# The first nine pairs of an attention-then-mixture kernel: another chunk border, merged mask and add instructions, some row sums on the tensor engine, dummy products, and a new order

## The chip, the cores and the metric

The kernel runs on one core of one Trainium2 chip. The core has five engines with queues of their own: PE (TensorE, matrix products; its weight loads are shown as PEld), DVE (VectorE), ACT (ScalarE), POOL (GpSimd) and SP (SyncE, which here only issues DMAs). The metric is device time in microseconds, from the first to the last instruction of one execution; the median of several executions is compared. All times below are microseconds (us) unless marked ns.

## The reference

Two attention layers follow each other. The first has 8 batches of 8 heads, 576 positions and head width 64, with a bias made of running sums; the second takes its output (576 x 512 per batch) through four experts, each a causal attention of head width 64, and adds the two experts that a gate picks.

```
scores = scale * q @ k.T ; s_pos = max(s, 0) ; cum = cumsum(s_pos)
scores = where(causal, -1e9, scores + min(-(cum_i - cum_j), 0))
attn = exp(scores - rowmax) ; attn /= sum(attn) + 1e-9 ; out = attn @ v
...
logits = x @ w_gate ; two largest per row, softmax of the two -> w
for e in range(4):
    q, k, v = x @ wq[e], x @ wk[e], x @ wv[e]
    a = softmax(causal(scale * q @ k.T)) ; ye = a @ v @ wo[e]
    out += (w of e, where picked) * ye
```

## The kernel before

Work goes by **pairs**: two heads of the first layer, or two experts of the second, are one pair, and there are 50 slots, 48 of which hold a pair (`pairs`). Pairs 0 to 3 are batch 0 of the first layer, 4 to 7 batch 1; pairs 8 and 9 are batch 0 of the second layer; then the pattern (four and two) repeats every six slots.

For one pair the steps are these. `hi` (h0 to h3, hc) makes the rounded copies Q2 and K2 on ACT. `maxima` (m0 to m5, tiles mx, L488) computes bf16 scores on PE, and M0 to M5 (L502) reduces them to row maxima on DVE, ten reductions a pair, each with a read of the accumulator. `minus_max` (mt, mA, mq) turns the maxima on PE (L522), copies them on ACT (L526) and sends them by DMA into a row of Q2. `lo` (lq, lk, l0 to l3) makes the low parts Q1 and K1: copies on POOL (L446, first three pairs) or by DMA, on ACT (L455, first nine pairs), and subtractions on DVE (L463, L468; those of pair 1 on POOL). `scores` (s0 to s6, L549 and L554) computes transposed scores in three chunks of 512 columns and a tail, for two heads each; E0 to E6 (L570, L581) is the exponential on ACT into the tile p (two buffers, pairs take turns). `below` (d0 to d3, all on POOL) masks the diagonal blocks with L591 and adds the key blocks up into r (L602 to L616), so that one product with ones gives row sums later (`sums`, L698, copied by L707). `pv` (v0 to v7, L647) is the product with the values on PE, copied out by V0, V1 (L661). `recip` and `norm` divide, and `projections` (L874) are the second layer's products.

Every engine takes its instructions strictly in the order in which the program issues them, so the order decides what waits for what. That order is written out by hand as a list of `slot:step` words: FILLING (up to slot 9), MIDDLE (six slots, repeated five times) and DRAINING. A step of slot n works for pair n (scores), n-1 (pv, sums), n+1 (maxima 3 to 5, low parts) or n+2 (maxima 0 to 2, hi). PE's results go to eight banks, which `take` and `give` hand round in that order.

Of the kernel before, what the change touches and what calls it, by code (L numbers as in the profile page):

```python
# [177 lines left out]
def order():  # L178

    def listed(text, n0=0):  # L180
        for x in text.split():
            n, step = x.split(":")
            yield n0 + int(n), step
# [997 lines left out]
```

## Time and profile before

| | |
|---|---|
| median of 3 runs | 666.05 us (663.31 to 669.95) |
| profiled execution, first to last instruction | 663.4 us |
| PE / PEld busy | 96% / 80% |
| DVE / ACT / POOL busy | 84% / 68% / 68% |
| granted clock of PE, mean | 0.993 |

The profiled execution is one of its own; its span is its time, there is nothing outside it, and it lies inside the range of the runs, 2.7 us under their median. Busy shares are of the whole span. A busy PE is not PE at its peak, since the ends of products are modelled. Queries of the trace by stretch, line, wait and time follow in the section of rows.

### The profile page before, as it was taken

The numbers are of one execution on the slowest core, as the hardware profiler recorded it, in microseconds if no ns is written. First come the engines' busy times: TensorE is split into PE (matmuls) and PEld (weight loads), VectorE is DVE, ScalarE is ACT, GpSimd is POOL, SyncE is SP. The second block draws the span as 40 slices with busy tenths as digits, with TensorE's granted clock in tenths as the row PEclk, the third lists the DMA queues.
The fourth block names the chain that finished last, engine by engine and source line by source line (L and its number), as shares of the span: only waits on it lengthen the run. The fifth ranks groups of instructions, "written<-read, shape, count | busy, mean of one in ns | idle before, by whom it ended". The sixth has DMA issues, their size and how long they took to land.

```text
span 663.4 us, 16171 instructions
## 1 busy us (share of the span) xinstructions
PE 637.9 (96%) x5792; PEld 528.1 (80%) x5792; DVE 559.4 (84%) x1446; ACT 454.3 (68%) x983; POOL 451.3 (68%) x611
## 2 busy tenths in 40 slices
PE   3889899999999999999999999999999999999997
PEld 1665698797897888788888888878887888779885
DVE  6889897998989898988989899897989976681985
ACT  6578868677667776777668766677767767566464
POOL 9889768678758667766786686686677766837030
PEclk9989999999999999999999999999999999999999
DMA  4435343544544473445643555535634543421323
GB/s 144 129 92 158 112 134 83 140 127 120 156 128 121 128 190 86 125 120 148 174 105 105 156 131 144 135 115 142 184 90 127 144 121 79 122 78 36 92 65 112
DMA packets 52157, 81.21 MB, mean 122 GB/s; under 512 B 18430, under 2 KB 26622, under 8 KB 52078
## 3 DMA queue, kind: packets, MB, share of 16 engines
q1 hardware_dynamic: 52078, 80.18, 44.5%
q8 instruction: 46, 0.75, 0.5%
q14 instruction: 33, 0.27, 0.1%
HBM read 44.55 MB, written 10.09 MB: 82 GB/s over the span
## 4 chain that ended last, share of the span: by engine, by line
PE 78%; DVE 9%; DMA 5%; ACT 4%; SPq 1%; issue 1%; DVEq 0%; ACTq 0%
PE pvp L647 15%; PE pq L874 13%; PE s L549 10%; PE s L554 10%; PE mx L488 8%; PE pw L874 8%; PE po L874 6%; PE sm L698 3%; DVE mx L502 3%; DVE k L468 1%; DMA q<-mr 1%; DVE pv L765 1%; PE po L850 1%; DMA k<-cum 1%; ACT k L431 1%
## 5 line engine op out<-in xcount | busy, mean ns | idle before, releaser
L502 DVE CUSTOM_DVE_ANT_0 mx<-mx,mask 128x64 f32<-128x64 f32 (+7 forms) x432 | 184.8, 445 | 42.5 <-PE mx L488 30.6
L570 ACT ACTIVATE p<-s 128x512 f32<-128x512 f32 x288 | 161.7, 594 | 66.8 <-PE s L554 62.5
L591 POOL TENSOR_SCALAR_AFFINE_SELECT p<-p 128x256 f32<-128x256 f32 (+1 forms) x240 | 124.1, 518 | 105.6 <-ACT p L570 96.9
L549 PE MATMUL s<-q,k 128*128 128x256 f32 (+3 forms) x672 | 175.1, 290 | 3.0 <-DVE mcol L502 2.4
L554 PE MATMUL s<-q,k 97*128 97x256 f32 (+3 forms) x672 | 164.8, 286 | 3.3 <-DMA q<-mr 3.2
L549 PEld LDWEIGHTS s<-q,k 128*128 128x128 f32 (+1 forms) x672 | 125.5, 187 | 13.3 <-issue 2.6
L613 POOL TENSOR_TENSOR r<-r,p 128x640 f32<-128x640 f32 x92 | 129.0, 1402 | 7.7
L554 PEld LDWEIGHTS s<-q,k 97*128 97x128 f32 (+1 forms) x672 | 124.7, 187 | 5.9 <-DMA q<-mr 4.7
L488 PE MATMUL mx<-k,q 96*64 96x320 bf16 (+7 forms) x960 | 97.5, 307 | 13.5 <-DMA k<-p 11.3
L647 PE MATMUL pvp<-p,v 128*64 128x320 f32 (+4 forms) x1024 | 105.6, 337 | 0.4 <-ACT mr L526 0.4
L463 DVE TENSOR_TENSOR q<-raw,q 64x576 fp32r<-64x576 f32 x94 | 84.2, 903 | 25.8 <-ACT q L428 11.9
L647 PEld LDWEIGHTS pvp<-p,v 128*64 128x64 f32 x1024 | 65.6, 137 | 32.1 <-issue 2.5
L468 DVE TENSOR_TENSOR k<-raw,k 64x576 fp32r<-64x576 f32 x94 | 86.3, 925 | 3.1 <-DMA k<-k 0.6
L488 PEld LDWEIGHTS <-q 96*64 96x64 bf16 x960 | 47.7, 114 | 42.3 <-issue 12.1
L874 PE MATMUL pq<-xh,wqkh 128*128 128x288 f32 x256 | 77.7, 303 | 0.1
L874 PE MATMUL pq<-xl,wqkh 128*128 128x288 f32 x256 | 75.5, 295 | 0.0
L874 PE MATMUL pq<-xh,wqkl 128*128 128x288 f32 x256 | 75.5, 295 | 0.0
L608 POOL TENSOR_TENSOR r<-p 128x256 f32<-128x256 f32 x46 | 36.3, 789 | 54.4 <-ACT p L570 53.8
L428 ACT ACTIVATE q<-raw 64x576 fp32r<-64x576 f32 x96 | 64.6, 679 | 6.7 <-DMA raw<-in_qk_dram 5.6
L502 DVE DVE_READ_ACCUMULATOR2_ANT mcol<- 128x1 f32 x480 | 65.7, 137 | 0.8
L431 ACT ACTIVATE k<-raw 64x576 fp32r<-64x576 f32 x96 | 64.3, 680 | 1.8
L661 ACT ACTIVATE pv<-pvp 128x256 f32<-128x256 f32 (+1 forms) x92 | 36.6, 406 | 28.4 <-PE pvp L647 28.4
(133 smaller groups left out, 1201.5 us busy)
## 6 DMA issues: line engine op xcount, KB each, us to landing
raw<-in_qk_dram SPq DMA_DIRECT2D x30, 576.0 KB
rb<-rr SPq DMA_DIRECT2D x92, 144.0 KB
q<-q SPq DMA_DIRECT2D x45, 288.0 KB
k<-k SPq DMA_DIRECT2D x39, 288.0 KB
v<-in_vm_dram SPq DMA_DIRECT2D x32, 256.0 KB
out_dram<-o SPq DMA_DIRECT2D x32, 256.0 KB
q<-mr SPq DMA_DIRECT2D x96, 2.2 KB
raw<-in_qk_dram SPq DMA_DIRECT2D x4, 288.0 KB
```

The lines of the kernel that those rows point to most:

```text
L431: nc.scalar.activation(k2[0:64, j], get_raw(n, j)[64:128], AF.Copy)
L463: eng.tensor_tensor(a[64:128, j], get_raw(n, j)[0:64], q2[0:64, j].bitcast(F32), op=OP.subtract)
L468: eng.tensor_tensor(c[0:64, j], get_raw(n, j)[64:128], c[64:128, j].bitcast(F32), op=OP.subtract)
L488: nc.tensor.matmul(t[64 * j : 64 * j + 64, c0 : c0 + k1 - k0], q2[0:RC, 64 * qt : 64 * qt + 64], k2[0:RC, k0:k1], start=True, stop=True,)
L502: nc.vector.tensor_tensor_reduce(t[:, c0 : c0 + w], t[:, c0 : c0 + w], mask[:, m0 : m0 + w], scale=1.0, scalar=mcol[n][:, 9:10] if slot == ...
L549: nc.tensor.matmul(t[0:nk, c0 : c0 + q1 - q0], K1[r1(n)][:, j, k0 : k0 + nk], Q1[r1(n)][:, j, q0:q1], start=True, stop=False,)
L554: nc.tensor.matmul(t[0:nk, c0 : c0 + q1 - q0], K2[r2(n)][0 : RM + 1, j, k0 : k0 + nk], Q2[r2(n)][0 : RM + 1, j, q0:q1], start=False, stop= ...
L570: nc.scalar.activation(ptile[n][:, x % 2, 512 * ci : 512 * ci + 512], tl[x], AF.Exp, scale=0.125)
L591: nc.gpsimd.affine_select(out=a, in_=a, pattern=[[0, 2], [1, nk]], compare_op=OP.is_ge, fill=0.0, base=0, channel_multiplier=-1,)
L613: add(r[:, :, q0:S], r[:, :, q0:S], p[:, :, 1024 + c : 1024 + c + S - q0], op=OP.add)
L647: nc.tensor.matmul(cur[h][64 * j : 64 * j + 64, q0 - PVC[h] : q1 - PVC[h]], vsl(j, kt), ptile[n][:, j, c : c + q1 - q0], start=first, stop ...
L874: nc.tensor.matmul(t[0:nk, 0:w], l, r, start=(x == 0), stop=(x == len(terms) - 1))
```

## The change

It touches the first nine pairs (EARLY = 9), and one thing in all pairs.

- Chunks: in pairs 0 to 8 the first two chunks of scores end at query column 320, not 256 and 576/384 (`EARLY_SCHUNKS`), and the value product's halves meet at 320 too. Columns in total stay the same.
- p is laid out anew: the two heads of a chunk lie beside each other, so that both diagonal masks of a chunk, for both heads, are one instruction (four blocks of 128). The third chunk's masks are merged so in every pair; the first chunk's in pairs 0 to 8.
- Adds: in pairs 0 to 8 the first chunk has one add (two heads of 192) and the second one (two of 256). The copy of the first 128 columns into r is a step of its own, e0: on POOL in pairs 0 to 3, on ACT in 4 to 8.
- Row sums: in pairs 0 to 3 (SUMMED = 4) POOL doesn't add the third chunk and the tail; PE sums r, the third chunk and the tail by products with ones (`early_sums`, b0), and ACT copies them out (B0). `sums` of those pairs falls away.
- Low parts: in pairs 0 to 8 both heads are one instruction (l0 and l1; l2 and l3 fall away). The K copy of pairs 3 to 8 moves from ACT to POOL, one instruction of 64 x 1152.
- Two fills of ring 0 move from POOL to DVE; the identity, the ones, gw and tlt move into unused columns of p.
- Dummy products: 12 of 256 columns before everything else and 48 of 64 columns (z0 to z47) spread over slots -2 to 4, all into one bank that is held until `zz`.
- Order: one list, STEPS. From 10:mq on it equals the old order word for word, apart from words that name no step.

```diff
+EARLY_SCHUNKS = [
+    [(0, 0, 320, 0), (1, 128, 320, 320)],
+    [(0, 320, 576, 0), (1, 320, 576, 256)],
+    [(2, 256, 576, 0), (3, 384, 576, 320)],
+]
+EARLY = 9
+SUMMED = 4
+FIRST_IDLE, IDLE = 12, 48
...
         def copy_k():
-            if n < COPY_K:
+            if COPY_Q <= n < COPY_K:
+                nc.gpsimd.tensor_scalar(
+                    c[64:128], get_raw(n, slice(0, 2))[64:128], 1.0, 0.0, op0=OP.mult, op1=OP.add
+                )
+            elif n < COPY_K:
...
-        for j in range(2):
+        parts = (slice(0, 2),) if n < EARLY else (0, 1)
+        for x, j in enumerate(parts):
...
+        def two_diags(ci):
+            base = PCHUNK[ci][0]
+            lower(p[:, base : base + 1280].rearrange("p (b c) -> p b c", c=320)[:, :, 0:128], 128)
...
+            if ci == 0 and n < EARLY:
+                two_diags(0)
+                add(r[:, :, 128:320], chunk_of(0, 128, 320), chunk_of(0, 320, 512), op=OP.add)
...
+            elif ci == 1 and n < EARLY:
+                add(r[:, :, 320:S], chunk_of(1, 0, 256), chunk_of(1, 256, 512), op=OP.add)
...
+                two_diags(2)
+                if n >= SUMMED:
+                    for kt, q0, _, c in chunks(n)[2]:
+                        add(r[:, :, q0:S], r[:, :, q0:S], chunk_of(2, c, c + S - q0), op=OP.add)
...
+        def early_sums():
+            t = tl[7] = take(f"es{n}")
+            r = rtile[n]
+            for h, (a, z) in enumerate(((0, 384), (384, S))):
+                parts = [(r, a, z)] + [
+                    (heads(p, at, c, c + q1 - q0), q0, q1)
+                    for kt in (2, 3, 4)
+                    for q0, q1, at, c in pieces(n, kt, max(KT[kt][0], a), z)
+                    if q0 < q1
+                ]
+                for x, (src, q0, q1) in enumerate(parts):
+                    for j in range(2):
+                        o = 64 * h + 32 * j
+                        rows = src[:, j, q0:q1] if x == 0 else src[:, j]
+                        nc.tensor.matmul(
+                            t[o : o + 32, q0 - a : q1 - a], ones[:, 0:32], rows,
+                            start=x == 0, stop=x == len(parts) - 1, tile_position=(0, o),
+                        )
...
+    def idle(k, cols=64):
+        if not idle_bank:
+            idle_bank.append(take("idle"))
+        w, m = (ident, P) if k % 2 else (ones, D)
+        nc.tensor.matmul(
+            idle_bank[0][0:m, 0:cols], w, ones[:, 0:1].to_broadcast([P, cols]),
+            start=True, stop=True,
+        )
...
+    for k in range(FIRST_IDLE):
+        idle(0, 256)
     running_sums()
```

How instructions stand on two engines, at the places of which the prediction speaks. On POOL, the work of pair 2 on its exponentials (tile p, buffer 0; r2 are its sums; k1 is the low part of K). Before:

```order
L608 TENSOR_TENSOR r2_672<-p0_106 128x2x128
L609 TENSOR_TENSOR r2_672<-p0_106 128x2x192
L591 AFFINE_SELECT p0_106<-p0_106 128x2x128
L613 TENSOR_TENSOR r2_672<-r2_672,p0_106 128x2x320
L591 AFFINE_SELECT p0_106<-p0_106 128x2x128
L613 TENSOR_TENSOR r2_672<-r2_672,p0_106 128x2x192
L591 AFFINE_SELECT p0_106<-p0_106 128x2x128
L602 TENSOR_SCALAR r2_672<-p0_106 128x2x128
L591 AFFINE_SELECT p0_106<-p0_106 128x2x128
L606 TENSOR_TENSOR r2_672<-p0_106 128x2x128
L591 AFFINE_SELECT p0_106<-p0_106 64x2x64
L616 TENSOR_TENSOR r2_672<-r2_672,p0_106 64x2x64
```

And in the changed kernel, from pair 2's first add on, to the start of pair 3 (p1):

```order
L744 TENSOR_TENSOR r2_718<-p0_74 128x2x192
L753 TENSOR_TENSOR r2_718<-p0_74 128x2x256
L715 AFFINE_SELECT p0_74<-p0_74 128x4x128
L735 TENSOR_SCALAR r2_718<-p0_74 128x2x128
L573 TENSOR_SCALAR k1_0_66<-raw4_427 64x1152
L715 AFFINE_SELECT p1_75<-p1_75 128x4x128
```

Six adds are two, four masks are two (the first stands just ahead of these rows), and the K copy of pair 4 now stands between pair 2 and pair 3.

On DVE, the start of the program, from the end of the running sums. Before:

```order
L298 TENSOR_TENSOR p1_107<-s_c_124,p1_107 64x576
L468 TENSOR_TENSOR k1_0_66<-raw0_130,k1_0_66 64x576 x2
L502 ISA mx0_0_145,mcol0_164<-mx0_0_145,mask_86 128x448
L502 ISA mcol0_164 128x1
L502 ISA mx0_0_145,mcol0_164<-mx0_0_145,mask_86 128x64
```

And in the changed kernel:

```order
L417 TENSOR_TENSOR p1_75<-s_c_133,p1_75 64x576
L592 TENSOR_TENSOR k1_0_66<-raw0_139,k1_0_66 64x1152
L587 TENSOR_TENSOR q1_0_64<-raw0_139,q2_0_68 64x1152
L627 ISA mx0_1_168,mcol0_192<-mx0_1_168,mask_86 128x384
L627 ISA mcol0_192 128x1
```

The low part of Q of pair 0 has moved ahead of the first maxima; before, it stood behind all ten of pair 0 and two of pair 1.

## Rows read from the trace of the kernel before

**Rows 1.** Busy time by stretch: us, engines (instructions), granted clock, DMA share, GB/s.
```profile
12.20:32.90 20.70, 18.09 (x98) 12.44 (x95) 17.18 (x62) 12.00 (x22) 17.52 (x34) 1.00 0.49 143
...
43.20:50.00 6.80, 6.80 (x41) 4.36 (x39) 5.50 (x15) 3.62 (x8) 4.93 (x7) 0.50 0.34 105
...
12.20:151.00 138.80, 131.36 (x1137) 102.28 (x1135) 121.62 (x325) 102.34 (x211) 108.87 (x150) 0.98 0.45 124
151.00:280.00 129.00, 128.50 (x1237) 108.46 (x1233) 117.14 (x298) 89.71 (x199) 94.04 (x121) 1.00 0.49 132
```

**Rows 2.** Waits from 12.2 to 151 us: us in total, times, longest.
```profile
DVE mx L502 <- PE mx L488: 8.4, 9, 2.0
```

**Rows 3.** Timeline of PE, parts up to 151 us: start, us, instruction, idle before.
```profile
10.78 3.28 PE L488 MATMUL mx<-k,q 96*64 96x448 bf16 x20 [10.78 <-DMA k<-p]
...
32.16 0.41 PE L549 MATMUL s<-q,k 128*128 128x256 f32 x1
32.37 0.41 PE L554 MATMUL s<-q,k 97*128 97x256 f32 x1
...
33.00 0.28 PE L549 MATMUL s<-q,k 128*128 128x256 f32 x1
33.12 0.28 PE L554 MATMUL s<-q,k 97*128 97x256 f32 x1
...
41.45 0.42 PE L554 MATMUL s<-q,k 97*128 97x320 f32 x1 [0.86 <-DMA q<-mr]
...
151.21 1.08 PE L488 MATMUL mx<-k,q 96*64 96x512 bf16 x12
```

**Rows 4.** Timeline of DVE, 9 to 52 us.
```profile
9.60 0.75 DVE L468 TENSOR_TENSOR k<-raw,k 64x576 fp32r<-64x576 f32 x1
12.24 0.63 DVE L502 CUSTOM_DVE_ANT_0 mx<-mx,mask 128x448 f32<-128x448 f32 x1 [1.89 <-PE mx L488]
...
18.31 2.63 DVE L463 TENSOR_TENSOR q<-raw,q 64x576 fp32r<-64x576 f32 x2
...
26.81 0.50 DVE L502 CUSTOM_DVE_ANT_0 mx<-mx,mask 128x320 f32<-128x320 f32 x1 [1.96 <-PE mx L488]
...
30.39 0.70 DVE L502 CUSTOM_DVE_ANT_0 mx<-mx,mask 128x512 f32<-128x512 f32 x1 [0.79 <-PE mx L488]
...
43.98 0.70 DVE L502 CUSTOM_DVE_ANT_0 mx<-mx,mask 128x512 f32<-128x512 f32 x1 [1.11 <-PE mx L488]
...
50.44 1.59 DVE L468 TENSOR_TENSOR k<-raw,k 64x576 fp32r<-64x576 f32 x1
```

**Rows 5.** Timeline of POOL, 41 to 51 us (pairs 1 and 2).
```profile
41.32 0.73 POOL L608 TENSOR_TENSOR r<-p 128x256 f32<-128x256 f32 x1 [0.66 <-ACT p L570]
42.01 1.01 POOL L609 TENSOR_TENSOR r<-p 128x384 f32<-128x384 f32 x1
42.98 0.41 POOL L591 TENSOR_SCALAR_AFFINE_SELECT p<-p 128x256 f32<-128x256 f32 x1
43.47 1.55 POOL L613 TENSOR_TENSOR r<-r,p 128x640 f32<-128x640 f32 x1
...
50.42 1.00 POOL L609 TENSOR_TENSOR r<-p 128x384 f32<-128x384 f32 x1
```

**Rows 6.** Groups on POOL by shape, whole run: count, busy us, mean ns, idle before.
```profile
L591 POOL TENSOR_SCALAR_AFFINE_SELECT p<-p 128x256 f32<-128x256 f32 x192 | 101.7, 530 | 96.9 <-ACT p L570 96.9
...
L616 POOL TENSOR_TENSOR r<-r,p 64x128 f32<-64x128 f32 x48 | 27.4, 572 | 8.2 <-DVE r L613 4.3
L602 POOL TENSOR_SCALAR r<-p 128x256 f32<-128x256 f32 x48 | 23.9, 498 | 4.2
...
L446 POOL TENSOR_SCALAR q<-raw 64x576 fp32r<-64x576 f32 x6 | 5.0, 842 | 0.2
```

**Rows 7.** Timeline of PE, 51 us: half of a quad's row sums, and what follows.
```profile
51.20 0.69 PE L698 MATMUL sm<-r,ones 128*32 128x288 f32 x8
51.83 0.65 PE L647 MATMUL pvp<-p,v 128*64 128x256 f32 x4
```

More of the change, by code (lines that the diff above doesn't have):

```diff
@@ L33, with chunks, pv_cols, pieces @@
 ]
-PCOLS = 1600
-LASTQ = [(0, 256), (256, 384), (384, 576)]
-PVC = [0, 256, 576]
-PT = 1536
-def pieces(kt, q0, q1):
+EARLY_SCHUNKS = [
[3 rows of a table added]
+]
+EARLY = 9
+SUMMED = 4
+FIRST_IDLE, IDLE = 12, 48
+PCHUNK = [(1152, 640), (2304, 512), (0, 640)]
+PTAIL = (512, 64)
+PSPARE = 1152 + 512
+PCOLS = 3328
+LASTQ = [(0, 256), (256, 384), (384, 576)]
+def chunks(n):
+    return EARLY_SCHUNKS if n < EARLY else SCHUNKS
+def pv_cols(n):
+    return [0, 320, 576] if n < EARLY else [0, 256, 576]
+def pieces(n, kt, q0, q1):
     if kt == 4:
-        return [(q0, q1, PT + q0 - 512)]
+        return [(q0, q1, PTAIL, q0 - 512)]
     out = []
-    for ci, segs in enumerate(SCHUNKS):
+    for ci, segs in enumerate(chunks(n)):
         for k, a, z, c in segs:
@@ L48, in pieces, with heads @@
             if k == kt and lo < hi:
-                out.append((lo, hi, 512 * ci + c + lo - a))
+                out.append((lo, hi, PCHUNK[ci], c + lo - a))
     return out
+def heads(t, at, c0, c1):
+    base, width = at
+    t = t[:, base : base + 2 * width].rearrange("p (j c) -> p j c", c=width)
+    return t[:, :, c0:c1]
 MBANKS = [
@@ L61 @@
 ]
-FILLING = (
[39 rows of a table removed]
-)
-MIDDLE = (
[24 rows of a table removed]
-)
-DRAINING = (
[43 rows of a table removed]
+STEPS = (
[213 rows of a table added]
 )
 def order():
[L180 to L183, printed above, removed]
-    yield from listed(FILLING)
-    for n0 in range(10, 40, 6):
-        yield from listed(MIDDLE, n0)
-    yield from listed(DRAINING)
+    for x in STEPS.split():
+        n, step = x.split(":")
+        yield int(n), step
 COPY_Q, COPY_K = 3, 9
@@ L215, in tile_attention_then_moe, with fill @@
     K2 = [const.tile([P, 2, S], F32R, tag=f"k2_{i}", name=f"k2_{i}") for i in range(NQK2)]
-    def fill(*rings):
-        for i in rings:
-            nc.gpsimd.memset(K2[i][64:96].bitcast(F32), 0.0)
-        for i in rings:
-            nc.gpsimd.memset(Q2[i][64:96].bitcast(F32), 1.0)
-        for i in rings:
-            nc.gpsimd.memset(K2[i][96:128].bitcast(F32), 1.0)
+    def fill(i):
+        eng = nc.gpsimd if i else nc.vector
+        eng.memset(K2[i][64:96].bitcast(F32), 0.0)
+        eng.memset(Q2[i][64:96].bitcast(F32), 1.0)
+        nc.gpsimd.memset(K2[i][96:128].bitcast(F32), 1.0)
+    PB = [const.tile([P, PCOLS], F32, tag=f"p{i}", name=f"p{i}") for i in range(2)]
+    ones = PB[1][:, PSPARE : PSPARE + D]
+    nc.vector.memset(ones, 1.0)
     fill(0)
-    ident = const.tile([P, P], F32, tag="ident", name="ident")
+    ident = PB[0][:, PSPARE : PSPARE + P]
     make_identity(nc, ident)
-    ones = const.tile([P, D], F32, tag="ones", name="ones")
-    nc.vector.memset(ones, 1.0)
+    gw = PB[1][:, PSPARE + D : PSPARE + D + 5 * E].rearrange("p (t e) -> p t e", e=E)
     eps = const.tile([P, 1], F32, tag="eps", name="eps")
@@ L254, in tile_attention_then_moe @@
     zL = const.tile([P, 2, P], F32R, tag="zl", name="zl")
-    PB = [const.tile([P, 2, PCOLS], F32, tag=f"p{i}", name=f"p{i}") for i in range(2)]
     VB = [const.tile([P, 2, 5, D], F32, tag=f"v{i}", name=f"v{i}") for i in range(3)]
     vx = const.tile([P, 5, 260], F32, tag="vx", name="vx")
-    gw = const.tile([P, 5, E], F32, tag="gw", name="gw")
-    tlt = const.tile([P, 5, E, E], BF16, tag="tlt", name="tlt")
+    tlt = PB[1][:, PSPARE + D + 5 * E : PSPARE + P - 4].bitcast(BF16)
+    tlt = tlt.rearrange("p (t a b) -> p t a b", a=E, b=E)
     tgt = const.tile([P, 5, E, E], BF16, tag="tgt", name="tgt")
@@ L266, in late_constants @@
         for i in range(2):
-            nc.gpsimd.memset(PB[i][64:128, :, PT:PCOLS], 0.0)
+            nc.gpsimd.memset(heads(PB[i], PTAIL, 0, 64)[64:128], 0.0)
         for i in range(3):
@@ L564, in chunk @@
             t = tl[x] = bank(x)
-            for kt, q0, q1, c0 in SCHUNKS[x // 2]:
+            for kt, q0, q1, c0 in chunks(n)[x // 2]:
                 seg(t, x % 2, kt, q0, q1, c0)
@@ L570, in exp @@
             nc.scalar.activation(
-                ptile[n][:, x % 2, 512 * ci : 512 * ci + 512], tl[x], AF.Exp, scale=0.125
+                heads(ptile[n], PCHUNK[ci], 0, 512)[:, x % 2], tl[x], AF.Exp, scale=0.125
             )
@@ L581, in exp_tail @@
             nc.scalar.activation(
-                ptile[n][0:64, :, PT:PCOLS],
+                heads(ptile[n], PTAIL, 0, 64)[0:64],
                 tl[6][0:64, 0:128].rearrange("p (j c) -> p j c", c=64), AF.Exp, scale=0.125,
@@ L585, in exp_tail, with lower @@
             give(tl[6])
-        def diag(kt):
-            nk = KT[kt][1]
-            (_, _, c), = pieces(kt, KT[kt][0], KT[kt][0] + nk)
-            a = ptile[n][0:nk, :, c : c + nk]
+        p = ptile[n]
+        def lower(a, w):
             nc.gpsimd.affine_select(
-                out=a, in_=a, pattern=[[0, 2], [1, nk]], compare_op=OP.is_ge,
+                out=a, in_=a, pattern=[[0, a.shape[1]], [1, w]], compare_op=OP.is_ge,
                 fill=0.0, base=0, channel_multiplier=-1,
             )
-        def below(ci):
+        def two_diags(ci):
+            base = PCHUNK[ci][0]
+            lower(p[:, base : base + 1280].rearrange("p (b c) -> p b c", c=320)[:, :, 0:128], 128)
@@ L597, in below, with chunk_of, sums_of, first @@
+        def chunk_of(ci, c0, c1):
+            return heads(p, PCHUNK[ci], c0, c1)
+        def sums_of():
             if n not in rtile:
                 rtile[n] = sb.tile([P, 2, S], F32, tag="r", name=f"r{n}", bufs=3)
-            p, r = ptile[n], rtile[n]
-            if ci == 0:
-                diag(0)
+            return rtile[n]
+        def first():
+            r, a = sums_of()[:, :, 0:128], chunk_of(0, 0, 128)
+            if n < SUMMED:
+                nc.gpsimd.tensor_scalar(r, a, 1.0, 0.0, op0=OP.mult, op1=OP.add)
+            else:
+                nc.scalar.activation(r, a, AF.Copy)
@@ L602, in below @@
+        def below(ci):
+            if ci < 2 or n >= SUMMED:
+                r = sums_of()
+            if ci == 0 and n < EARLY:
+                two_diags(0)
+                add(r[:, :, 128:320], chunk_of(0, 128, 320), chunk_of(0, 320, 512), op=OP.add)
+            elif ci == 0:
+                lower(chunk_of(0, 0, 128), 128)
                 nc.gpsimd.tensor_scalar(
-                    r[:, :, 0:128], p[:, :, 0:128], 1.0, 0.0, op0=OP.mult, op1=OP.add
+                    r[:, :, 0:128], chunk_of(0, 0, 128), 1.0, 0.0, op0=OP.mult, op1=OP.add
@@ L604, in below @@
                 )
-                diag(1)
-                add(r[:, :, 128:256], p[:, :, 128:256], p[:, :, 256:384], op=OP.add)
+                lower(chunk_of(0, 256, 384), 128)
+                add(r[:, :, 128:256], chunk_of(0, 128, 256), chunk_of(0, 256, 384), op=OP.add)
+            elif ci == 1 and n < EARLY:
+                add(r[:, :, 320:S], chunk_of(1, 0, 256), chunk_of(1, 256, 512), op=OP.add)
             elif ci == 1:
-                add(r[:, :, 256:384], p[:, :, 512:640], p[:, :, 384:512], op=OP.add)
@@ L609, in below @@
[L609 removed]
+                add(r[:, :, 256:384], chunk_of(1, 0, 128), chunk_of(0, 384, 512), op=OP.add)
+                add(r[:, :, 384:S], chunk_of(1, 128, 320), chunk_of(1, 320, 512), op=OP.add)
             elif ci == 2:
[L611 to L617 removed]
+                two_diags(2)
@@ new lines, in below @@
+                if n >= SUMMED:
+                    for kt, q0, _, c in chunks(n)[2]:
+                        add(r[:, :, q0:S], r[:, :, q0:S], chunk_of(2, c, c + S - q0), op=OP.add)
+            else:
+                a = heads(p, PTAIL, 0, 64)[0:64]
+                lower(a, 64)
+                if n >= SUMMED:
+                    nc.gpsimd.tensor_tensor(r[0:64, :, 512:S], r[0:64, :, 512:S], a, op=OP.add)
+        def early_sums():
[16 more added lines that the diff above has]
+                        )
@@ L618, in below, with early_copy @@
+        def early_copy():
+            m = n | 1
+            if m not in rs:
+                rs[m] = sb.tile([P, S], F32, tag="rs", name=f"rs{m}", bufs=1)
+            o = 64 * (n % 2)
+            for h, (a, z) in enumerate(((0, 384), (384, S))):
+                nc.scalar.activation(
+                    rs[m][o : o + 64, a:z], tl[7][64 * h : 64 * h + 64, 0 : z - a],
+                    AF.Identity, bias=eps[0:64],
                 )
+            give(tl[7])
         for x in range(6):
@@ L625, in scores @@
             items[f"d{ci}"] = lambda ci=ci: below(ci)
+        if n < EARLY:
+            items["e0"] = first
+        if n < SUMMED:
+            items["b0"] = early_sums
+            items["B0"] = early_copy
         return items
@@ L632, in pv @@
         ph, b, i = pairs[n]
+        PVC = pv_cols(n)
         items = {}
@@ L648, in piece @@
                     cur[h][64 * j : 64 * j + 64, q0 - PVC[h] : q1 - PVC[h]],
-                    vsl(j, kt), ptile[n][:, j, c : c + q1 - q0],
+                    vsl(j, kt), heads(ptile[n], at, c, c + q1 - q0)[:, j],
                     start=first, stop=fin,
@@ L669, in pv @@
                 for kt in kts
-                for q0, q1, _ in pieces(kt, max(KT[kt][0], PVC[h]), PVC[h + 1])
+                for q0, q1, *_ in pieces(n, kt, max(KT[kt][0], PVC[h]), PVC[h + 1])
             ]
@@ L687, in sums @@
     def sums(n):
-        if n not in quads:
+        if n not in quads or n < SUMMED:
             return {}
@@ L1127, in slot @@
                     steps.update(norm(z))
+        if n == -2 and IDLE:
+            for k in range(IDLE):
+                steps[f"z{k}"] = lambda k=k: idle(k)
+            steps["zz"] = lambda: give(idle_bank[0])
         if n == -1:
```

16 lines of the change are left out of this document (5 added, 11 removed), and 319 rows, old and new, of tables (DRAINING, FILLING, MIDDLE, STEPS).

## Prediction

> **What bounds the kernel now.** I read the busy time by stretch first. From 151 to 280 us PE is busy 128.50 of 129.00 us: the repeating middle part is paced by PE, nothing in it hangs on absolute time, and the order there is unchanged. So whatever the first slots win or lose arrives at the end one to one, and only the stretch up to about 151 us, where the new order meets the old one (10:mq; the first products behind it are in a group that starts at 151.21 us [rows 3]), has to be priced. In that stretch, 12.2 to 151 us, no engine is full: PE 131.36 of 138.80, DVE 121.62, POOL 108.87, ACT 102.34 [rows 1]. But PE's busy time is stretched. Products of 256 columns start 0.21 us apart at 32.2 us and 0.12 us apart at 33.0 us [rows 3]: up to about 32.9 us, from the first product at 10.78 us on [rows 3], PE ran at the lower of its two levels, 1.2 GHz, though the column of the granted clock says 1.00 for that stretch (no record of it was kept). From 43.2 to 50 us the granted clock is 0.50, the lower level again, and PE is busy all the 6.80 us [rows 1]; before that fall it had waited 0.86 us for a DMA [rows 3]. DVE is the engine with the least to spare behind it: 88% busy here, against 91% (117.14 of 129.00) in the steady part [rows 1]. Of its 17.2 us of idle time, 8.4 are waits for the maxima's products on PE [rows 2], and the rows of its timeline show where: 1.96 and 0.79 us at 26.8 and 30.4 us, 1.11 at 44.0, all in the two stretches at 1.2 GHz, and 1.89 us at 12.2 us, ahead of the first maxima [rows 4]. POOL is idle for 30 of the 138.8 us [rows 1] and is not last at the meeting point. My reading: DVE paces slots 0 to 5 and PE, by its projections, the rest, with the slow clock as the common cause of DVE's larger gaps.
>
> **The change, part by part.** I price it by DVE's time up to the meeting point, and then ask whether PE and POOL follow.
>
> Start on DVE. The Q low part of pair 0 moves ahead of the first maxima, into the 1.89 us in which DVE waited for PE. Uncontended, a 64x576 subtraction takes 0.75 us [rows 4], so two take 1.5 us, and they fit. Later, where the two stood, 2.63 us come free [rows 4], of which 1.1 us were contention that may come back elsewhere. I take 1.5 us won (0 to 1.9).
>
> Clock. The dummy products are to keep PE at 2.4 GHz from its first real product. If they do, the three DVE waits of 1.96, 0.79 and 1.11 us go: 3.9 us (0 to 3.9, and to 8.4 if all waits on PE went).
>
> Low parts. Eight pairs (0 and 2 to 8; pair 1's run on POOL) have two DVE instructions where four stood: 16 fewer. What one costs beside its elements: the reductions of 320 and 512 columns take 0.50 and 0.70 us [rows 4], which is 1.04 ns a column, so 576 columns are 0.60 us, and 0.15 of the 0.75 us is fixed. 16 x 0.15 = 2.4 us. The slope is that of another operation; ends 0 and 4.8 us (twice the fixed part).
>
> POOL. In pairs 0 to 3 the adds of 0.73 (L608), 0.73 (L606, same size), 1.01, 1.55, 1.01 and 0.57 us, 5.6 us, become one of 1.01 (two of 192) and one of two of 256: from 0.73 at 256 and 1.01 at 384 elements, 1.29 at 512. That is 3.3 us a pair, 13.2 in four. In pairs 4 to 8, 0.73 + 0.73 + 1.01 become 2.3 and a copy of 0.50 us goes to ACT: 0.7 a pair, 3.3. A double mask has no row; between 0.41 (no dearer) and 0.82 I take 0.6, so 0.2 saved twice a pair, 3.6 us in nine. Against it six K copies of 64x1152: two of L446 would be 1.7 us; 1.5 each, 9 us [rows 5, 6]. POOL's 108.87 us fall by about 11. With its 30 us of idle time this is cover and not gain: it lets value products of pairs 0 to 3 start earlier, and I price it at nothing by itself (0 to 3 us). What is queued behind each K copy are the next pair's masks, and behind those PE's value products; 1.5 us six times is less than the 13 us taken off ahead of them.
>
> ACT loses 12 K copies and gets five copies and some more sum copies; with 36 us idle [rows 1] it stays off the path. Nothing.
>
> PE. Half a quad's row sums, 288 columns with four groups side by side, hold PE 0.63 us (51.20 to 51.83) [rows 7]: 2.2 ns a column. A pair's early sums stream 1152 columns a head: 2.5 us if only the two heads run side by side, half if all four groups do. Four pairs: 5 to 10 us, less the two quads' old sums (2 x 2 x 0.63 = 2.5): 2.5 to 7.6 more. The dummies of 64 columns cost 0.14 us each at that price; some 40 stand behind the first real product: 5.6 us. The 12 of 256 columns are 0.56 us each, 6.7 us, twice that at the lower level; they run before 10.78 us, where PE had nothing to do [rows 3], and at worst delay the first maxima by about 2 us. So PE gets at most 13 us more, and the clock gives back half of what was busy at the lower level: 18.09 / 2 + 6.80 / 2 = 12.4 us [rows 1]. The two cancel; I take 0, with ends 0 and 6 us lost. One bank of eight is held by the dummies up to slot 4; no row prices that, and I put it into the same ends.
>
> Everything behind slot 10: the third chunk's masks are merged in all pairs, but POOL waits there anyway (96.9 us idle ahead of L591 in the whole run, for exponentials [rows 6]): nothing.
>
> The port. At 50.44 us a DVE subtraction took 1.59 us instead of 0.75 beside a POOL add that had started at 50.42 and took 1.00 [rows 4, 5]: it waited for about that add's end. Half as many DVE subtractions and less POOL work mean fewer such meetings, six K copies mean new ones; I take 0, from 2 won to 9 lost. The Trainium skill, "SBUF — State Buffer", section "SBUF: two separate sides", calls the pair of ports that VectorE and GpSimd share an exclusive lock, held for the whole instruction, for a VectorE operation with two SBUF inputs against a GpSimd one that reads SBUF; the trace agrees in this row (0.84 us lost of 1.00). By that rule moving copies from ACT to POOL speaks against this change; the second rival below is what it would make.
>
> **Sum.** 1.5 + 3.9 + 2.4 = 7.8 us off the profiled execution's 663.4, so 655.6. That execution is one run, 2.7 us under the median of the three shown, so against the median: 666.05 - 7.8 = 658.
>
> **Rivals.** 1% of 666 is 6.7 us, about what a measurement of this kernel can tell from no change, since its runs spread from 663.3 to 670.
>
> Forecast: DVE closes its gaps, 658 us, own range 653 to 661. For it: the gaps are named and two of the three causes are removed. Against it: the gaps of one order are replaced by those of another, and a kernel whose first slots have four engines at 74 to 95% seldom loses a gap without growing one.
>
> The port takes it back: each of the six K copies on POOL (1.3 to 1.7 us) stands close to the DVE subtraction that reads it, in the neighbouring pair's work. If every one blocks a subtraction of the other stream for its length, 9 us are lost; for half of them 4.5: 666.05 - 7.8 + 4.5 = 663. For it: the 1.59 and 2.63 us rows. Against it: two operations must meet in time, and of the rows of 0.75 us and more [rows 4] one ran at 9.60 us undisturbed.
>
> The change doesn't do what it says: the sparse dummies don't keep the clock up, the waits of 3.9 us stay: 662. For it: PE fell to the lower level at 43.2 us after a stretch with only short waits; between the first maxima and the first scores, 12 to 20 us, the new PE queue is still sparse.
>
> Slower: PE becomes the engine that paces slots 0 to 4. The place is PE's queue, where sums and dummies stand ahead of products that are ready. At the lower level the 13 us added are 26; nothing is given back; what PE had free in the stretch is 7.4 us (138.80 - 131.36), and DVE then waits, so its savings are worth nothing: 26 - 7.4 = 19 us, 685. It decides from the point where the added time less what the clock returns is over 7.4 us. Against it: at 2.4 GHz the difference is under 1 us.
>
> **How the numbers follow.** Forecast 0.50, the port 0.23, the clock 0.20, slower 0.07. The first is faster by over 1%, the next two within 1%, the last slower: 0.50, 0.43, 0.07. The range: at best DVE is 95% busy, (121.6 - 2.4) / 0.95 = 125.5 us instead of 138.8, 13.3 won, and with the runs' spread 651; at the other end both middle rivals together, and half of PE's bound, 668.
>
> **What the profile would show.** If right: products of 256 columns 0.12 us apart from the first scores on and no stretch with a granted clock of 0.50; the group of maxima's products at the meeting point (151.21 us before) near 143.5; DVE's waits for the maxima's products before it under 5 us; POOL's busy time up to there near 98 us; the span behind it unchanged within 2 us. The prediction is wrong if DVE's waits name another cause in the same size, if subtractions on DVE average well over 2 x 0.75 us for both heads, or if the part behind the meeting point gets longer.

## The result and the profile after

| | before | after |
|---|---|---|
| median of 15 runs | 667.96 us (663.31 to 669.95) | 662.12 us (660.07 to 666.38) |
| ratio | | 0.9917, 95% interval 0.9898 to 0.9937 |
| profiled execution | 663.4 us | 662.1 us |

The change wins 5.8 us. That is clear of the noise, and with 0.8% it is below the 1% that I had named as what can be told from no change. A run's time and its profiled span are not the same: the profiled run of after is listed with 663.8 us and spans 662.1, and in all runs with both numbers the time is 1.7 to 2.2 us above the span. So something lies outside the span, and a span of 663.4 us stands for a run of before of about 665.1, 2.9 us under its median and among its fastest; the one of after lies 1.7 us over its median. The two profiles differ by only 1.3 us. A comparison of the two shows what the fill became, and not where the medians part.

The windows of after that answer to [rows 1] (us, engines with instructions, granted clock), and three more, cut where its clock changes:

```profile
12.20:32.90 20.70, 20.70 (x130) 16.41 (x125) 14.21 (x49) 10.56 (x20) 12.29 (x9) 0.59 0.26 68
43.20:50.00 6.80, 6.80 (x67) 5.94 (x63) 6.08 (x10) 5.80 (x13) 2.96 (x4) 1.00 0.64 209
12.20:151.00 138.80, 135.50 (x1261) 114.60 (x1255) 115.66 (x308) 99.01 (x207) 90.40 (x105) 0.93 0.46 123
151.00:280.00 129.00, 128.68 (x1245) 109.02 (x1245) 114.09 (x294) 89.56 (x199) 91.29 (x113) 1.00 0.48 129
...
12.40:29.30 16.90, 16.90 (x91) 13.20 (x87) 10.75 (x44) 7.67 (x15) 8.68 (x6) 0.50 0.22 58
29.40:142.00 112.60, 109.30 (x1107) 92.30 (x1107) 96.09 (x244) 85.58 (x182) 77.30 (x94) 1.00 0.50 134
142.10:145.40 3.30, 3.30 (x18) 3.30 (x17) 3.23 (x11) 1.96 (x4) 3.03 (x4) 0.50 0.79 200
```

The record of the clock begins at 5.5 us, at 2.4 GHz, while the first burst of dummies runs, and falls at 12.3 us, just behind the first maxima (11.10 us). Then PE is busy all of 16.90 us, dummies included, and all of it at 1.2 GHz. Behind that, one fall of 3.3 us is left up to 151 us. POOL is down to 90.40 us from 108.87, DVE to 115.66 from 121.62. PE is up by only 4.1 us. DVE, which was to close its gaps, has more of them: 23.1 us idle of the 138.8 where before had 17.2. PE has 3.3 where it had 7.4.

The timeline of PE in after, parts up to the meeting point, answers to [rows 3]:

```profile
20.54 0.45 PE L1273 MATMUL idle<-p 128*64 128x64 f32 x2
...
22.57 0.48 PE L1273 MATMUL idle<-p 128*64 128x64 f32 x2
22.98 0.64 PE L674 MATMUL s<-q,k 128*128 128x320 f32 x1
...
28.00 0.41 PE L674 MATMUL s<-q,k 128*128 128x256 f32 x1
28.21 0.41 PE L679 MATMUL s<-q,k 97*128 97x256 f32 x1
...
32.54 0.28 PE L679 MATMUL s<-q,k 97*128 97x256 f32 x1
32.66 0.28 PE L674 MATMUL s<-q,k 128*128 128x256 f32 x1
...
152.18 1.34 PE L613 MATMUL mx<-k,q 96*64 96x448 bf16 x16
```

Five dummies hold PE for 2.44 us (20.54 to 22.98) directly ahead of pair 0's first scores, which came at 19.21 us in the trace of before. Products of 256 columns are still 0.21 us apart at 28.0 us, 0.12 at 32.5. The group of pair 12's maxima at the meeting point starts at 152.18 us (151.21 before), but the two groups do not hold the same products. The first scores of pair 12 do, in before and then in after:

```profile
168.03 0.31 PE L549 MATMUL s<-q,k 128*128 128x320 f32 x1
169.77 0.31 PE L674 MATMUL s<-q,k 128*128 128x320 f32 x1
```

They come 1.7 us later in after, and from them to the end it is 495.3 and 492.3 us. So in this pair of profiles the fill has won nothing, and what is won lies behind it.

DVE in after, timeline (answering to [rows 4]) and then its longest waits from 12.2 to 151 us (to [rows 2]; total, times, longest):

```profile
9.34 1.41 DVE L592 TENSOR_TENSOR k<-raw,k 64x1152 fp32r<-64x1152 f32 x1 [0.33 <-ACT k L578]
10.78 1.35 DVE L587 TENSOR_TENSOR q<-raw,q 64x1152 fp32r<-64x1152 f32 x1
12.43 0.57 DVE L627 CUSTOM_DVE_ANT_0 mx<-mx,mask 128x384 f32<-128x384 f32 x1 [0.29 <-PE mx L613]
...
29.41 2.48 DVE L587 TENSOR_TENSOR q<-raw,q 64x1152 fp32r<-64x1152 f32 x1 [5.63 <-ACT p L695]
```
```profile
DVE q L587 <- ACT p L695: 5.6, 1, 5.6
DVE mx L627 <- PE mx L613: 3.5, 4, 1.7
DVE wol L436 <- ACT woh L435: 3.4, 1, 3.4
```

The waits for the maxima's products fell from 8.4 to 3.5 us as hoped. A new one stands in their place: Q's low part of pair 2 needs the ring of two to be read out by pair 0's scores. The last of those starts at 29.12 us, and DVE's queue stands behind it. (The row names an exponential on ACT as what came last; the readers of the ring are the scores.)

### The profile page after: what moved, and what is told of

The parts are those of the page before. It is cut to its first block, busy times and chain, and to the rows that moved or that the text cites. A ratio compares the mean times of both kernels' runs of the same rounds, so it can differ in the third digit from the quotient of the medians.

```text
span 662.1 us, 16453 instructions
## 1 busy us (share of the span) xinstructions
PE 650.7 (98%) x5976; PEld 547.3 (83%) x5976; DVE 558.2 (84%) x1432; ACT 450.3 (68%) x980; POOL 424.4 (64%) x530
## 4 chain that ended last, share of the span: by engine, by line
PE 81%; DVE 7%; DMA 4%; ACT 3%; issue 2%; SPq 1%; DVEq 0%; ACTq 0%
PE pvp L832 16%; PE pq L1058 12%; PE s L674 11%; PE s L679 10%; PE pw L1058 9%; PE mx L613 9%; PE po L1058 7%; PE sm L882 3%; DVE mx L627 3%; PE idle L1273 1%; DMA rb<-rr 1%; ACT p L695 1%; DVE pv L949 1%; DMA raw<-in_qk_dram 1%; PE po L1034 1%
## 5 line engine op out<-in xcount | busy, mean ns | idle before, releaser
L715 POOL TENSOR_SCALAR_AFFINE_SELECT p<-p 64x128 f32<-64x128 f32 (+2 forms) x183 | 111.7, 611 | 117.8 <-ACT p L695 103.2
L674 PE MATMUL s<-q,k 128*128 128x320 f32 (+3 forms) x672 | 173.5, 288 | 2.3 <-DVE mcol L627 2.2
L679 PE MATMUL s<-q,k 97*128 97x320 f32 (+3 forms) x672 | 163.8, 285 | 0.6 <-DMA q<-mr 0.6
L761 POOL TENSOR_TENSOR r<-r,p 128x640 f32<-128x640 f32 x84 | 118.0, 1405 | 6.8
L587 DVE TENSOR_TENSOR q<-raw,q 64x576 fp32r<-64x576 f32 (+1 forms) x86 | 82.8, 971 | 25.7 <-ACT q L547 11.9
L832 PE MATMUL pvp<-p,v 128*64 128x192 f32 (+4 forms) x1024 | 102.2, 334 | 0.8 <-DVE mcol L627 0.8
L613 PE MATMUL mx<-k,q 96*64 96x448 bf16 (+6 forms) x960 | 92.6, 300 | 1.8 <-DMA k<-p 0.9
L592 DVE TENSOR_TENSOR k<-raw,k 64x576 fp32r<-64x576 f32 (+1 forms) x86 | 87.1, 1020 | 2.6 <-ACT k L578 0.3
L755 POOL TENSOR_TENSOR r<-p 128x256 f32<-128x256 f32 x37 | 28.9, 780 | 52.6 <-ACT p L695 52.1
L846 ACT ACTIVATE pv<-pvp 128x320 f32<-128x320 f32 (+1 forms) x92 | 36.4, 405 | 27.5 <-PE pvp L832 27.4
```

Source lines behind the costliest of these rows:

```text
L587: eng.tensor_tensor(a[64:128, j], get_raw(n, j)[0:64], q2[0:64, j].bitcast(F32), op=OP.subtract)
L592: eng.tensor_tensor(c[0:64, j], get_raw(n, j)[64:128], c[64:128, j].bitcast(F32), op=OP.subtract)
L613: nc.tensor.matmul(t[64 * j : 64 * j + 64, c0 : c0 + k1 - k0], q2[0:RC, 64 * qt : 64 * qt + 64], k2[0:RC, k0:k1], start=True, stop=True,)
L674: nc.tensor.matmul(t[0:nk, c0 : c0 + q1 - q0], K1[r1(n)][:, j, k0 : k0 + nk], Q1[r1(n)][:, j, q0:q1], start=True, stop=False,)
L679: nc.tensor.matmul(t[0:nk, c0 : c0 + q1 - q0], K2[r2(n)][0 : RM + 1, j, k0 : k0 + nk], Q2[r2(n)][0 : RM + 1, j, q0:q1], start=False, stop= ...
L715: nc.gpsimd.affine_select(out=a, in_=a, pattern=[[0, a.shape[1]], [1, w]], compare_op=OP.is_ge, fill=0.0, base=0, channel_multiplier=-1,)
```

## The experiments

Ratios are to the kernel before, run on the same chip beside each kernel, with 95% intervals. Kernels e1 to e4 shared a chip, e5 to e8 another, e9 to e11 a third; e12 ran by itself.

**e1, the kernel before again** (no edit). 

> The kernel before, once more, for a second profiled execution. In the pair of profiles at hand pair 12's first scores come at 168.0 us before and 169.8 after, though the medians differ by 5.8 us the other way. Theory fill (the change wins its time in the first nine pairs, and the profile of before was a lucky one): with a span near 666, pair 12's first scores stand at 171 us or later, and the distance from there to the end is the same 495.4 us within 1. Theory behind (the time is won behind pair 10, by the third chunk's merged masks): pair 12's first scores stand within 1.5 us of 168.0 again, and what is longer lies behind them.

It took 669.1 us (ratio 1.0031, 0.9993 to 1.0068); the profiled span is 667.6 us. Two windows of its trace:

```profile
43.20:50.00 6.80, 5.49 (x50) 3.09 (x48) 6.00 (x18) 4.62 (x11) 6.55 (x8) 1.00 0.48 132
68.50:75.20 6.70, 6.70 (x37) 5.15 (x35) 5.53 (x14) 4.56 (x12) 0.49 (x1) 0.50 0.46 149
```

The fall that [rows 1] had at 43.2 us is gone, and one as long stands at 68.5 us, where PE is busy throughout. Pair 12's first scores come at 171.4 us, 3.3 us later than in the first profile, and from there to the end it is 496.3 against 495.3 us, within the 1 us expected. So these two executions of the kernel before differ in their fill, and what is seen to differ there is where the clock falls. That the change wins its time in the fill does not follow: against this second profile after is 5.5 us shorter, and only 1.6 us of it lie ahead of pair 12's first scores.

**e2, no dummies.** 

> The kernel after without any dummy product; their PSUM bank joins the rotation. Theory dummies hold the clock: without them TensorE stays at 1.2 GHz up to about 33 us and falls again later, as before; 3 to 8 us are lost, ratio to the kernel before 0.997 to 1.003. Theory dummies only cost: in the profile of after the clock fell at 11.1 us in spite of them, and five of 0.4 us each stand ahead of pair 0's first scores; without them those scores come 2 to 3 us earlier and the kernel is 1 to 3 us faster than after, ratio to before 0.987 to 0.990.

```diff
-FIRST_IDLE, IDLE = 12, 48
+FIRST_IDLE, IDLE = 0, 0
```

658.5 us, ratio 0.9863 (0.9823 to 0.9903). Its timeline of PE has the first scores at 20.07 us:

```profile
18.39 1.76 PE L613 MATMUL mx<-k,q 96*64 96x384 bf16 x14
20.07 0.64 PE L674 MATMUL s<-q,k 128*128 128x320 f32 x1
```

So the dummies cost, about 3.6 us by the two ratios. The profiled execution itself was the slowest of its six (663.5 us); I read its start from it, and nothing of its total.

**e3, Q's low part of pair 2 later.** 

> The kernel after with one instruction moved: Q's low part of pair 2, which waited 5.6 us for pair 0's last scores with VectorE's queue behind it, stands behind the maxima of pair 2 instead of ahead of their last four banks. Theory VectorE paces the fill: it saves up to 3.9 us (the reductions that now stand in the gap: 31.82 to 35.8), ratio to before 0.986 to 0.989. Theory PE at 1.2 GHz paces the first 28 us: the wait is filled but pair 2's scores come no more than 1 us earlier, ratio as of after, 0.9917.

```diff
-... 0:m2 1:l0 0:E2 ... 0:M2 1:s6 ...
+... 0:m2 0:E2 ... 0:M2 1:l0 1:s6 ...
```

661.1 us, ratio 0.9906 (0.9875 to 0.9937), not to be told from after. The timeline of DVE says why:

```profile
30.59 0.70 DVE L627 CUSTOM_DVE_ANT_0 mx<-mx,mask 128x512 f32<-128x512 f32 x1 [6.52 <-PE mx L613]
```

The instruction that now comes first waits 6.52 us for PE instead of 5.63. Pair 2's scores come at 44.1 us (43.8 in after). The new wait was cover; PE at 1.2 GHz paces the first 28 us, not DVE.

**e4, the third chunk's masks apart again from pair 9 on.** 

> The kernel after with the third chunk's two masks as instructions of their own again in pairs 9 to 48, in the order of the kernel before; the first nine pairs keep everything. Theory behind: the 5.8 us go, ratio to before 0.998 to 1.002. Theory fill: no change against after, ratio 0.990 to 0.993. Half each: 0.995.

```diff
-                two_diags(2)
+                if n < EARLY:
+                    two_diags(2)
                 if n >= SUMMED:
                     for kt, q0, _, c in chunks(n)[2]:
+                        if n >= EARLY:
+                            lower(chunk_of(2, c, c + 128), 128)
                         add(r[:, :, q0:S], r[:, :, q0:S], chunk_of(2, c, c + S - q0), op=OP.add)
```

662.9 us, ratio 0.9916 (0.9888 to 0.9944): as after. Behind the meeting point the change is worth nothing.

**e5 and e6, one kind of dummies each.** 

> The kernel after with only the 12 dummies of 256 columns ahead of everything, none of 64. Theory A: the 64-column dummies cost, since they stand in PE's queue ahead of products while the clock is low (pair 0's first scores 22.98 us after, 20.07 with no dummy at all); then this kernel is as fast as the one without any, 658 to 659, ratio to before 0.985 to 0.988. Theory B: it is the first burst that costs, because it delays the start or sets the clock's later falls; then the ratio is that of after, 0.990 to 0.992.

> The kernel after with only the 48 dummies of 64 columns, without the first burst. Theory A (the 64-column ones cost): ratio as of after, 0.990 to 0.992, pair 0's first scores near 23 us. Theory B (the first burst costs): ratio 0.985 to 0.988. If both together are needed to lose anything, both kernels stand at 0.986.

```diff
 e5
-FIRST_IDLE, IDLE = 12, 48
+FIRST_IDLE, IDLE = 12, 0
...
+    give(idle_bank[0])
 e6
-FIRST_IDLE, IDLE = 12, 48
+FIRST_IDLE, IDLE = 0, 48
```

e5: 659.3 us, ratio 0.9853 (0.9807 to 0.9899). e6: 663.3 us, 0.9922 (0.9891 to 0.9953). On one chip 4.0 us lie between them. Theory A holds: the 48 dummies of 64 columns cost, the first burst doesn't. One thing goes with them: e5 gives the dummies' bank back right behind the burst, e6 and after hold it up to slot 4, and no run separates the two. In after's trace PE is idle for 1.8 us between 12.2 and 100 us, so waits for a bank can hardly make more than that of the 4.0. In e5's trace, an execution of 653.8 us and the fastest of its six, the windows show what the start can be:

```profile
13.90:24.10 10.20, 8.25 (x45) 6.32 (x46) 9.00 (x40) 3.32 (x7) 7.28 (x4) 0.50 0.23 65
24.20:151.00 126.80, 122.25 (x1216) 101.33 (x1216) 110.69 (x289) 97.47 (x208) 92.87 (x109) 1.00 0.49 132
```

Here the clock is up from 24.2 us on, 5 us earlier than in after, with no fall up to the meeting point, though PE was idle for 2 of the 10 us at the lower level. Pair 12's maxima start some 10 us earlier than in after. One trace is not the rule: in e10's, with the same burst, the clock came up at 25.5 us, and in e7's, with all dummies, at 26.0. In e2's, its slowest, it came up at 34.1 us and pair 12's first scores at 168.9, against 160.0 in e5's; yet the medians of e2 and e5 are alike.

**e7, K copies of pairs 3 to 8 on ACT again.** 

> The kernel after with the six K copies of pairs 3 to 8 back on ScalarE, two instructions each, at the same places of the order. Theory port: on POOL they block VectorE's low parts for some of their 1.5 us (the 2.3 us subtraction at 38.9 us); away from it VectorE wins up to 4.5 us, ratio to before 0.985 to 0.990. Theory cover: POOL's K copies only spare ScalarE; with them back nothing changes up to 1 us, ratio 0.991 to 0.993, or ScalarE becomes late in slots 3 to 8 and it is 1 to 4 us slower, 0.993 to 0.998.

```diff
-            if COPY_Q <= n < COPY_K:
+            if False:
```

663.0 us, ratio 0.9912 (0.9880 to 0.9945): cover, as after. DVE's low parts between 9 and 110 us hardly get shorter either; K's and Q's together are busy 23.3 us here and 23.7 in after, 15 instructions each. Meetings there are, in after on DVE and then on POOL:

```profile
38.86 2.32 DVE L592 TENSOR_TENSOR k<-raw,k 64x1152 fp32r<-64x1152 f32 x1
```
```profile
38.68 1.28 POOL L753 TENSOR_TENSOR r<-p 128x512 f32<-128x512 f32 x1
40.05 2.15 POOL L573 TENSOR_SCALAR k<-raw 64x1152 fp32r<-64x1152 f32 x1
```

The subtraction starts while an add runs and takes 2.32 us instead of 1.35; the K copy behind that add starts while the subtraction runs and takes 2.15 us, where the one at 63.13 us took 1.15. In e7 the same subtraction takes 2.38 us at 37.20 us, beside an add and a mask: without the K copy it meets something else. The Trainium skill, "SBUF — State Buffer", section "SBUF: two separate sides", calls the pair of ports that VectorE and GpSimd share an exclusive lock, held for the whole instruction. The rows above agree with it; that K copies on POOL therefore cost time in the end, as the prediction's rival had it, no run shows.

**e8, low parts as two instructions again, at the same places.** 

> The kernel after with the low parts of the first nine pairs as one instruction for each head again, at the same places. Theory of the forecast: 16 instructions more on VectorE at 0.15 us each, 2.4 us, arrive at the end, ratio to before 0.995. Rival: VectorE has slack where they stand (it waited 5.6 us at 29.4), nothing arrives, ratio 0.991 to 0.992; or the shorter instructions give the port back sooner and a part of the 2.3 to 2.5 us ones goes, ratio 0.989 to 0.991.

```diff
             def f2(j=j):
-                eng.tensor_tensor(
-                    a[64:128, j], ...
+                for j in (0, 1) if n < EARLY else (j,):
+                    eng.tensor_tensor(
+                        a[64:128, j], ...
...
```

665.9 us, ratio 0.9976 (0.9944 to 1.0008). After did not run on this chip; by the two ratios e8 is 3.9 us slower. Beside e7, which did but differs from e8 in its K copies too, it is 3.0. So merging is worth 3 to 4 us, more than half of the gain. Groups on DVE between 9 and 110 us (busy, mean ns), of after and then of e8:

```profile
L592 DVE TENSOR_TENSOR k<-raw,k 64x1152 fp32r<-64x1152 f32 x8 | 12.9, 1616 | 0.5 <-ACT k L578 0.3
L587 DVE TENSOR_TENSOR q<-raw,q 64x1152 fp32r<-64x1152 f32 x7 | 10.8, 1541 | 5.8 <-ACT p L695 5.6
```
```profile
L594 DVE TENSOR_TENSOR k<-raw,k 64x576 fp32r<-64x576 f32 x14 | 14.8, 1098 | 0.2
L588 DVE TENSOR_TENSOR q<-raw,q 64x576 fp32r<-64x576 f32 x14 | 12.2, 909 | 5.1 <-ACT p L697 4.9
...
10.80 1.42 DVE L588 TENSOR_TENSOR q<-raw,q 64x576 fp32r<-64x576 f32 x2
```

Undisturbed, two apart take 1.42 us (the last row, of the timeline) and one merged 1.35: 0.07 us. In the mean two apart take 2 x 0.96 = 1.93 us and one merged 1.58: 0.35 us, 16 times 5.6. In both traces every subtraction longer than undisturbed overlaps an instruction of POOL in time, ten of 28 in e8 and seven of 15 in after. So merging pays hardly by the fixed cost, and mostly by fewer instructions that meet one of POOL's.

**e9 and e12, row sums of pairs 0 to 3 as before.** 

> The kernel after with the row sums of pairs 0 to 3 made as before: GpSimd adds the third chunk and the tail into the sums tile (as soon as all five steps of a pair are done), and TensorE sums a whole pair of pairs, at the places where the early sums of pairs 1 and 3 stood. Theory cover: GpSimd's 10 us are cover, VectorE is not waiting for them; ratio as of after, 0.991 to 0.993. Theory GpSimd: the port and the waits of the value products behind GpSimd's masks were what the early sums took away; without them 2 to 5 us are lost, 0.995 to 0.999. Theory PE: the early sums cost PE more than they give; 1 to 3 us are won, 0.987 to 0.990.

```diff
-SUMMED = 4
+SUMMED = 0
...
-    "1:b0 3:m3 -2:z38 3:m4 1:B0 ...
+    "2:a0 2:a1 3:m3 -2:z38 3:m4 2:A0 2:A1 ...
-    "3:v2 3:m0 2:b0 3:b0 ... 3:B0 "
+    "3:v2 3:m0 2:b0 4:a0 4:a1 ... 4:A0 4:A1 "
...
+            if not left:
+                r = sums_of()
+                for kt, q0, _, c in chunks(n)[2]:
+                    add(r[:, :, q0:S], r[:, :, q0:S], chunk_of(2, c, c + S - q0), op=OP.add)
+                a = heads(p, PTAIL, 0, 64)[0:64]
+                add(r[0:64, :, 512:S], r[0:64, :, 512:S], a, op=OP.add)
```

677.4 us, ratio 1.0155 (1.0114 to 1.0197), some 16 us over after. PE waited for GpSimd's adds at the early places:

```profile
71.21 1.19 PE L897 MATMUL sm<-r,p 128*32 128x288 f32 x8 [4.07 <-POOL r L776]
```

So in e12 the sums were moved back to about where the kernel before has them (edit against e9). 

> The kernel with the row sums of pairs 0 to 3 made as before, with one thing moved: TensorE's halves for pairs 0 and 1 stand behind the value products of pair 2 and those for pairs 2 and 3 behind pair 4's first scores, about where the kernel before has them. With them at the early places TensorE waited 4.07 and 1.80 us for GpSimd's adds (71.2 to 74.2 us) and the kernel took 677.4 us. Theory place: the 15 us were these waits in PE's queue; here it is within 3 us of after, ratio to before 0.992 to 0.997. Theory GpSimd: with the third chunk's adds GpSimd is busy 24.04 of 25 us between 50 and 75 us, the exponentials' buffers and the value products behind it come late wherever the sums stand; 4 us or more are lost against after, ratio 0.999 to 1.012.

```diff
-    "2:a0 2:a1 3:m3 ... 2:A0 2:A1 ... 2:V1 2:m0 3:s1 3:s0 ... 4:a0 4:a1 ... 4:A0 4:A1 ... 4:s0 4:E0 3:n0
+    "3:m3 ... 2:V1 2:m0 2:a0 2:a1 3:s1 3:s0 2:A0 2:A1 ... 4:s0 4:E0 4:a0 4:a1 4:A0 4:A1 3:n0
```

676.6 us, ratio 1.0133 (1.0079 to 1.0187), some 14 us over after. Theory place falls: the wait of 4.07 us is gone and the time is not. Theory GpSimd, a loss of 4 us or more wherever the sums stand, holds by what it forecast, though not in its size. The window of 50 to 75 us in after, and then in e12:

```profile
50.00:75.00 25.00, 25.00 (x291) 20.66 (x292) 20.14 (x57) 20.17 (x41) 16.00 (x18) 1.00 0.50 141
```
```profile
50.00:75.00 25.00, 20.30 (x203) 15.16 (x200) 21.23 (x46) 16.63 (x32) 24.04 (x24) 1.00 0.32 94
```

With the sums on GpSimd, POOL is full (24.04 of 25.00 us) and PE has holes; without them PE is full and POOL has 9 us to spare. What PE waits for between 40 and 100 us in e12 is of several kinds:

```profile
PE pvp L847 <- POOL v L388: 2.3, 1, 2.3
PE sm L897 <- POOL r L778: 2.0, 1, 2.0
PE mx L613 <- DVE mcol L627: 1.7, 2, 0.9
PE s L674 <- DVE k L592: 1.5, 1, 1.5
```

The first two rows are POOL's own, and the fourth is K's low part on DVE, which reads a K copy that POOL makes. Behind such waits the clock falls too, two windows of e12's trace (where after has 1.00 in both):

```profile
30.00:50.00 20.00, 17.73 (x155) 14.87 (x155) 16.32 (x41) 13.38 (x27) 19.15 (x32) 0.91 0.51 150
75.00:100.00 25.00, 22.07 (x195) 19.28 (x196) 19.41 (x47) 15.21 (x33) 13.90 (x14) 0.93 0.65 162
```

Over runs the mean clock of e12 has a median of 0.9755 where after has 0.986, with records that begin alike: up to 7 us of the 14, if PE paced all of it. How much is POOL's queue by itself is not shown. Sums as before together with K copies on ACT were not tried, nor the adds right behind their masks, as the kernel before has them; e9 and e12 add them in one block behind a pair's last mask.

**e10, first burst alone and Q's low part of pair 2 later.** 

> The kernel after with the first burst of 12 dummies alone (none of 64 columns), and Q's low part of pair 2 behind the maxima of pair 2. If the two edits add up: the burst alone stood at 0.9853, the moved low part won 0 to 1 us, so 0.982 to 0.986. If VectorE paces once the 64-column dummies are gone, the moved low part is worth more than it was beside them, 2 to 4 us: 0.979 to 0.982. If the wait is PE's in either case: 0.985 to 0.987.

The edit is that of e5 and that of e3. 658.0 us, ratio 0.9879 (0.9828 to 0.9930): no better than e5, the moved instruction gives nothing here either. e2, e5 and e10 are the kernels that beat both.

**e11, the kernel before with the first burst.** 

> The kernel before with the burst of 12 dummies of 256 columns in front, nothing else. Theory burst: in the profile of the kernel after with the burst alone the clock rose to 2.4 GHz at 24.1 us, against 30 to 34 us in the kernels without a burst; if the burst does this whatever the order behind it, the kernel before wins 2 to 5 us by it, ratio 0.993 to 0.997. Theory order: the earlier rise came from the denser order of the first slots; the burst alone does nothing here, 0.998 to 1.002.

```diff
+    t = take("idle")
+    for k in range(12):
+        nc.tensor.matmul(
+            t[0:D, 0:256], ones, ones[:, 0:1].to_broadcast([P, 256]),
+            start=True, stop=True,
+        )
+    give(t)
     running_sums()
```

666.7 us, ratio 0.9997 (0.9967 to 1.0028). Theory order, as far as the time goes: the burst alone does nothing. In its trace the clock comes up at 30.1 us, against 33.0 and 30.9 in the two of before.

## Why the prediction was right, and where its steps were not

The range held the time, faster came, and the size was 5.8 us against a sum of 7.8. The mechanism did not hold, and by the prediction's own classes the outcome is one of the 0.43 (within 1%) and not of the 0.50. Its frame was that DVE paces slots 0 to 5 and closes its gaps. DVE's idle time grew from 17.2 to 23.1 us; its waits for the maxima fell from 8.4 to 3.5, but a wait of 5.6 us with another cause came in their place, which the prediction had named as a sign of being wrong; and e3 shows that this wait was cover, with PE at the lower level the slower engine. Of the six signs that a profile was to show, one came (waits for the maxima under 5 us). That the time came near the forecast is in part luck, since errors of several us cancelled. One sum is off as well: the upper end of the range, both middle rivals and half of PE's bound, is over 669 by its own terms and not 668.

**Clock, 3.9 us.** This step failed: the rival "sparse dummies don't keep the clock up" came in its place. Its mechanism came; that its 662 was hit as well is luck of the base. On the median of fifteen runs of before the rival is 664.1 and the forecast 660.2, and 662.1 lies between them. From 12.3 us on PE ran 17 us at 1.2 GHz in after, and products of 256 columns were 0.12 us apart only behind 29.4 us. What did change is later: the second fall of [rows 1] is gone in the profile of after, and e1 shows that such a fall wanders in the kernel before. Over runs it can be read from the mean clock of kernels whose record begins alike, near 30 us: median 0.991 in the 25 runs of before that stood beside e6, 0.997 in e6's ten. 0.6% of 669 us are 4.0 us where PE paces, much of the 5.9 us between these two medians. It isn't the dummies' doing: without any, e2's six runs have a median of 0.9965. Why the new order has fewer falls stays open.

**Dummies, priced at 5.6 us on PE and cancelled.** Mis-sized, and the cancelling failed. Five took 2.44 us ahead of the first scores, 0.49 each, where I had 0.14; with the clock low nothing gave that back. e5 against e6 puts the 48, with the bank that they hold, at 4.0 us of the whole. My slower rival had the place right, PE's queue in slots 0 to 4, and priced it at 19 us.

**Low parts, 2.4 us.** The mechanism was half right, the size low: 3.0 us by e8 against e7, 3.9 against after. The fixed cost that I took from the reductions, 0.15 us an instruction, is 0.07 us a merged pair; the rest is meetings with POOL, which I had left in the port's term at 0.

**Start on DVE, 1.5 us.** The step held on DVE: both low parts of pair 0 are done at 12.1 us, and the first reduction starts at 12.43 (12.24 before). It isn't seen further on: in after PE's dummies hold the first scores, and in e2, without any, they start at 20.07 us (19.21 before). No run separates it.

**POOL, 0.** This step failed by the most. I called POOL's relief cover, worth 0 to 3 us; e9 and e12 show that in this order it carries some 14 us, with the falls of the clock that its lack brings. In the kernel before POOL has 20.64 of 25 us between 50 and 75 us, and its sums fit there; my reading, not shown, is that the new order leaves no room for them beside six K copies, so that part of the change's worth was spent to pay for its other parts. POOL's busy time up to 151 us fell by 18.5 us, where I had summed 11. ACT at 0 and the K copies on POOL at 0 (e7) held, and so the port rival falls: 0 of its 4.5 us.

**Behind slot 10, 0.** For the merged masks this held: e4 is as after. The premise that all is won or lost up to 151 us did not hold to better than some 2 us. From pair 12's first scores to the end it is 494.0 to 496.3 us in the three traces of the old order (before, e1, e11) and 490.9 to 494.7 in those of the new one, e12 alone left out (497.0); in the first pair of profiles it shrank by 3.0, outside the 2 that I had allowed. The order there is the same and e4 has 492.8, so no merged mask did it. The cause stays open.

**The base.** Of the 4.1 us between the forecast of 658 and the time, 1.9 are the median before, 666.05 of three runs and 667.96 of fifteen; the other 2 are the gain's. And of the 2.7 us by which the profiled execution seemed to lie under its median, 1.7 are the time outside the span, which I had taken for nothing.
